# Windowed attention and a gated MLP on one core: the Wo load and the Q reads move to other places in one DMA queue

## The chip, the cores and the metric

The kernel runs on one core of a Trainium2 chip. The metric is the device time of one execution in microseconds (us). A profile is one execution taken by the hardware profiler; its span goes from the first to the last instruction of the program. In what follows PE is the matmul engine and PEld its weight loads, DVE the vector engine, ACT the scalar engine, POOL the GpSimd engine. SP is the engine that only issues DMAs and waits for semaphores: here nearly all DMAs go through its queue, in the order of the program, and while it waits for one of them everything behind it stands.

## What is computed

One block of a transformer on 2048 rows of 640 columns, in bf16: a layernorm, then attention with 32 heads of 20 columns in which each row sees the 256 rows up to and with itself, and beside it a gated MLP of width 1536. Both are added to the input.

```python
def _A_ref(x, wqkv, wo):
    qkv = (x @ wqkv).reshape(B, S, 3, H, Dh).transpose(2, 0, 3, 1, 4)
    q, k, v = qkv[0], qkv[1], qkv[2]
    scores = jnp.einsum("bhqd,bhkd->bhqk", q, k) * (Dh ** -0.5)
    mask = (idx[:, None] - idx[None, :] >= 0) & (idx[:, None] - idx[None, :] < W)
    p = _softmax(jnp.where(mask[None, None], scores, -1e9), axis=-1)
    o = jnp.einsum("bhqk,bhkd->bhqd", p, v)
    return o.transpose(0, 2, 1, 3).reshape(B, S, D) @ wo

def _B_ref(x, w_gate, w_up, w_down):
    h = _sigmoid(einsum("bsd,df->bsf", x, w_gate)) * einsum("bsd,df->bsf", x, w_up)
    return jnp.einsum("bsf,fd->bsd", h, w_down)

xn = _layernorm(x)
return x + _A_ref(xn, wqkv, wo) + _B_ref(xn, w_gate, w_up, w_down)
```

## The kernel before

The rows are cut into four chunks of 512. For each chunk the kernel makes, on PE, the projections to Q and K (`g_qk`, L366: five blocks `m` of 128 columns for Q, then five for K), the projection to V (`g_v`, L385), the gate and up products of the MLP (`g_gu`, L407), and at the end the down product and the output projection with Wo (`g_out`, L463, with `down`, L430, and `add_wo`, L437). The attention runs in steps of scores (`scores`, L480) and exponentials, followed two steps later by the product with V (`pv`, L508). A class `Fill` (L551) holds the other work as generators and deals it out between the score steps, so that PE always has something to do; the list of parts is at L689 to L707. The order of all instructions on each engine is thereby written out by the program itself; `tc.manual_schedule()` (L132) leaves it so, and adds only the semaphore waits.

Q and K come out of PE as 32 heads of 20 rows in a packed layout, and the scores need every head on partitions of its own. So each block goes through memory. `proj_block` (L292) copies a PSUM block to a tile `st` (Q on DVE, L301; K on ACT, L303) and stores it to a scratch tensor in device memory, `sq` or `sk` (L305). `spread` (L307) reads the scratch back into the tiles `qT` and `kT` (L315), two groups of four heads in each DMA of 256 KB. A read must wait until the stores that it reads have landed. A chunk has ten stores, four reads for the first half of the heads and four for the second half.

Wo needs its rows in another order as well: `turn_wo` (L209) writes them to the scratch tensor `wo_i`, and `load_wo` (L215) reads them into the tile `wo`, in four DMAs of 200 KB, one for each quarter of the partitions. The first matmuls that read `wo` are those of L439 in the output part of the first chunk.

The order of DMAs in SP's queue around the change, for the second chunk (c = 1):

- four stores of Q, the four loads of `wo` (L375), the fifth store of Q, two stores of K
- the two reads of `qT` for the first half (L377, yielded behind block m = 1 of K), three stores of K
- the two reads of `kT` for the first half (L393, L394, issued in `g_v`), then two of `qT` and two of `kT` for the second half (L396, L397)
- two loads of input rows (`new_rows`, L449, which the output part of the first chunk starts with)

For the third and fourth chunk it is the same without the loads of `wo`. The first chunk has an order of its own (L379 to L383, L195).

Each DMA that SP issues takes one of eight semaphores in turn, so a DMA also waits for the one issued eight places before it, where that is not known to have landed.

The programs of the engines are themselves in device memory and are brought in by DMA: in the page's list of queues these are the ones of kind "instruction".

Of the kernel before, what the change touches and what calls it, by code (L numbers as in the profile page):

```python
# [15 lines left out]
DC = D // P  # L16
# [77 lines left out]
def kernel(  # L94
# [42 lines left out]
    def load_x(c):  # L137
        t = xp.tile([P, SBC, D], BF16, name="xc")
        xc[c] = t
        nc.sync.dma_start(out=t, in_=xr[:, c * SBC:(c + 1) * SBC, :])  # L140
# [39 lines left out]
    def load_gu(t, w, k, lo=0, hi=FS):  # L180
        nc.sync.dma_start(out=t[k][:, :, lo:hi],
                          in_=w.rearrange("(c p) f -> p c f", p=P)[:, :, k * FS + lo:k * FS + hi])
# [32 lines left out]
    def load_wo():  # L215
        for i in range(HG):
            nc.sync.dma_start(out=wo[32 * i:32 * i + 32, :, :],
                              in_=wo_i[i].rearrange("(m j) n -> j m n", j=32))
# [73 lines left out]
    def proj_block(w, c, m):  # L292

        ps = ps_d.tile([P, CW], FP32, name="pqk", tag="d")
        for d in range(DC):
            wt = wqkv["qk".index(w)][:, d, :].rearrange("p (k m) -> p m k", m=DC)
            nc.tensor.matmul(ps, lhsT=wt[:, m, :], rhs=xnT[c][:, d, :],  # L297
                             start=(d == 0), stop=(d == DC - 1))
        st = stp.tile([P, CW], BF16, name="st")
        if w == "q":  # L300
            nc.vector.tensor_copy(out=st, in_=ps)  # L301
        else:
            nc.scalar.copy(out=st, in_=ps)  # L303
        dst = scratch[w, c % 2].rearrange("(h j) s -> h j s", j=32)
        nc.sync.dma_start(out=dst[:, 4 * m:4 * m + 4, :], in_=st)  # L305

    def spread(w, c, g0, g1):  # L307

        half, first = divmod(g0, GH)
        if first == 0:  # L310
            qk[w, c, half] = (qp if w == "q" else kp).tile([P, GH, CW], BF16, name=w + "T")
        src = scratch[w, c % 2].rearrange("(a b p) s -> b p a s", a=2, p=P)
        for b in range(g0 // 2, g1 // 2):
            o = 2 * b - half * GH
            nc.sync.dma_start(out=qk[w, c, half][:, o:o + 2, :], in_=src[b])  # L315

    def new_v(c, s):
        v = vp.tile([P, 2, VH], BF16, name="v")
        vt[c * SBC + s] = v
        nc.gpsimd.memset(v[:, :, 0:16 * VW].rearrange("p k (h d) -> p k h d", d=VW)[:, :, :, DH:VW], 0.5)  # L320
        nc.gpsimd.memset(v[:, :, 16 * VW:], 0.0)
# [16 lines left out]
    def proj_v(c, s, hf, copy):  # L338
        copy_v(c, s, hf, project_v(c, s, hf), copy)
# [26 lines left out]
    def g_qk(c):  # L366
        for w in "qk":
            for m in range(DC):
                proj_block(w, c, m)
                if c == 0 and w == "q" and m == 1:  # L370
                    load_x(1)
                if c == 0 and w == "q" and m == 3:
                    load_gu(wu, B_w_up, 0, FS // 2)
                if c == 1 and w == "q" and m == 3:
                    load_wo()  # L375
                if c and w == "k" and m == 1:
                    spread("q", c, 0, GH)  # L377
                yield 5 * MM
        if c == 0:  # L379
            spread("q", c, 0, 2)  # L380
            spread("k", c, 0, 2)
            spread("q", c, 2, 4)
            spread("k", c, 2, 4)  # L383

    def g_v(c):  # L385
        for s in range(SBC):
            new_v(c, s)
            for hf in range(2):
                proj_v(c, s, hf, nc.scalar.copy if hf else nc.vector.tensor_copy)
                if hf == 0:  # L390
                    yield 5 * 136
            if s == 0:
                spread("k", c, 0, 2)  # L393
                spread("k", c, 2, GH)  # L394
            if s == 1:
                spread("q", c, GH, NG)  # L396
                spread("k", c, GH, NG)  # L397
            yield 5 * 136


# [271 lines left out]
    for _ in g_qk(0):  # L672
        pass
# [19 lines left out]
    fill.add("wd", later(load_wd), 0)  # L693
    fill.add("pads", later(clear_next), 0)
    fill.add("qk1", g_qk(1), 50 * MM)
    fill.add("v1", mix(g_v(1), g_gu(1, 0, 2), 1, 2), 40 * 136 + 2 * GU)
    fill.add("out0", mix(g_out(0, g_gu(1, 2, 3)), norms2, 1, 1), OUT + GU)
    fill.add("x3", later(load_x, 3), 0)
    fill.add("qk2", g_qk(2), 50 * MM)
    fill.add("v2", mix(g_v(2), g_gu(1, 3, 7), 0, 1), 40 * 136 + 4 * GU)  # L700
    fill.add("gu1b", mix(g_gu(1, 7, 12), norms3, 0, 1, False), 5 * GU)
    fill.add("out1", mix(g_out(1, g_gu(2, 0, 1)), itertools.chain(norms3, g_turns(3)), 1, 2), OUT + GU)
    fill.add("qk3", g_qk(3), 50 * MM)
    fill.add("v3", mix(g_v(3), g_gu(2, 1, 5), 0, 1), 40 * 136 + 4 * GU)
    fill.add("gu2", g_gu(2, 5, 12), 7 * GU)
    fill.add("out2", g_out(2, (), g_gu(3, 0, 1)), OUT + GU)
# [37 lines left out]
    c = NCH - 1  # L744
# [62 lines left out]
```

## Time and profile before

| | us |
|---|---|
| median of three runs | 309.28 |
| lowest and highest of them | 309.27, 309.58 |
| the profiled execution, its own time | 309.91 |
| its span | 308.2 |

| engine | busy, us | share of the span |
|---|---|---|
| PE | 300.0 | 97% |
| ACT | 198.4 | 64% |
| DVE | 170.7 | 55% |
| POOL | 168.7 | 55% |

The granted clock of TensorE is 1.000 over the whole span. The DMA engines move 35.68 MB, 116 GB/s in the mean; by the page's 40 slices they are loaded to 4 to 9 tenths nearly throughout the first 85 us, and after that in bursts, with slices of 0 to 7 tenths. The wait table lists 3.3 us of waits on PE, 2.4 us of them on the warm-up and the transposes at the start (L232, L279). Since PE is busy to 97%, the table of engines says little more; what is of interest is the few places where PE stands, and the time of each DMA in SP's queue, which the timeline gives by its issue.

### The profile page before, as it was taken

To read this page: it belongs to the slowest core of one execution; us is meant where nothing else is said; L and a number is where in the kernel's file an instruction comes from. 1 tells how busy PE (TensorE), PEld (TensorE's weight loads), DVE (VectorE), ACT (ScalarE), POOL (GpSimd) and SP (SyncE) were. 2 spreads that over 40 slices of the span, in tenths; PEclk is the share of its full clock that TensorE was granted. 3 is DMA by queue.
4 is the path that set the end of the run, shared out by engine and by line. 5 is a ranking of instruction groups with operands and counts; after the bars stand their busy time and mean duration, and the time that the engine had idled before them with its cause. 6 is when DMAs were issued, how large, how long until landed. Compare 5 with 4: busy or idle time off the path is not lost.

```text
span 308.2 us, 9938 instructions
## 1 busy us (share of the span) xinstructions
PE 300.0 (97%) x4276; PEld 167.5 (54%) x4311; DVE 170.7 (55%) x339; ACT 198.4 (64%) x197; POOL 168.7 (55%) x308
## 2 busy tenths in 40 slices
PE   6999999999999999999999999999999999999995
PEld 2654444545556655554557664554546664444774
DVE  4733657648698364496947154383734536373423
ACT  5933777698854549888674647878585547678000
POOL 6000687687873937666682728557372837566000
PEclk9999999999999999999999999999999999999999
DMA  7997996984707353730002712650000200000202
GB/s 223 366 307 236 325 174 188 356 231 137 245 3 132 64 178 103 219 100 2 3 3 66 130 57 71 204 184 0 3 2 2 82 31 21 2 2 2 87 21 67
DMA packets 40460, 35.68 MB, mean 116 GB/s; under 512 B 10560, under 2 KB 39872, under 8 KB 40384
## 3 DMA queue, kind: packets, MB, share of 16 engines
q1 hardware_dynamic: 39552, 34.27, 37.8%
q10 hardware_dynamic: 864, 0.77, 0.8%
q8 instruction: 34, 0.56, 0.7%
q14 instruction: 10, 0.08, 0.1%
HBM read 23.63 MB, written 10.26 MB: 110 GB/s over the span
## 4 chain that ended last, share of the span: by engine, by line
PE 96%; DMA 1%; issue 1%; DVE 1%; ACT 0%; SPq 0%
PE y L432 18%; PE pu L418 17%; PE pg L411 17%; PE pqk L297 14%; PE ps L487 9%; PE pv L326 7%; PE y L439 7%; PE acc L520 6%; DMA xc<-in_A_x_dram 1%; PE pt L279 0%; ACT xn L617 0%; DVE xn L272 0%; DVE xn L628 0%; DVE stats L252 0%; SPq L156 0%
## 5 line engine op out<-in xcount | busy, mean ns | idle before, releaser
L504 POOL TENSOR_SCALAR_AFFINE_SELECT pT<-pT 64x512 bf16<-64x512 bf16 (+1 forms) x256 | 157.2, 614 | 109.8 <-ACT pT L493 97.3
L493 ACT ACTIVATE pT<-ps 128x2048 bf16<-128x2048 f32 (+1 forms) x76 | 141.0, 1855 | 59.9 <-PE ps L487 58.1
L422 DVE SCALAR_TENSOR_TENSOR h<-th,pu 128x512 bf16<-128x512 f32 x48 | 32.8, 683 | 52.9 <-PE pu L418 46.3
L418 PE MATMUL pu<-xnT,wu 128*128 128x512 bf16 x228 | 59.0, 380 | 0.7 <-issue 0.2
L411 PE MATMUL pg<-xnT,wg 128*128 128x512 bf16 x226 | 58.5, 380 | 0.9 <-issue 0.3
L432 PE MATMUL y<-wd,h 128*128 128x320 bf16 (+2 forms) x396 | 56.8, 295 | 0.2 <-issue 0.2
L432 PEld LDWEIGHTS <-h 128*128 128x128 bf16 x396 | 36.7, 98 | 16.1 <-issue 2.3
L414 ACT ACTIVATE th<-pg 128x512 f32<-128x512 f32 x48 | 28.6, 595 | 15.5 <-PE pg L411 15.4
L411 PEld LDWEIGHTS <-wg 128*128 128x128 bf16 x240 | 22.3, 98 | 25.8 <-issue 2.0
L418 PEld LDWEIGHTS <-wu 128*128 128x128 bf16 x240 | 22.0, 98 | 25.5 <-issue 2.0
L487 PE MATMUL ps<-qT,kT 20*64 20x320 bf16 (+4 forms) x1440 | 32.1, 260 | 0.0
L532 DVE STREAM_TRANSPOSE t<-acc 128x512 f32<-128x512 f32 x32 | 21.1, 696 | 19.4 <-PE acc L520 19.2
L487 PEld LDWEIGHTS <-kT 20*64 20x64 bf16 x1440 | 15.4, 103 | 24.8 <-issue 21.8
L443 DVE SCALAR_TENSOR_TENSOR rows<-y,rows 128x320 bf16<-128x320 f32 x30 | 14.4, 488 | 25.5 <-PE y L439 25.4
L544 DVE TENSOR_TENSOR on<-t,rec 128x320 bf16<-128x320 f32 (+4 forms) x48 | 27.8, 579 | 1.1
L326 PE MATMUL pv<-wv,xnT 128*128 128x320 bf16 x160 | 25.8, 300 | 0.0
L439 PE MATMUL y<-wo,oc 128*128 128x320 bf16 (+2 forms) x165 | 24.2, 295 | 0.0
L297 PE MATMUL pqk<-xnT,wk 128*128 128x512 bf16 x97 | 23.1, 381 | 0.2
L297 PE MATMUL pqk<-xnT,wq 128*128 128x512 bf16 x94 | 22.8, 381 | 0.4 <-issue 0.2
L335 DVE CAST v<-pv 64x320 bf16<-64x320 f32 x29 | 14.1, 486 | 12.5 <-PE pv L326 12.3
L520 PE MATMUL acc<-pT,v 64*32 64x320 bf16 (+4 forms) x1440 | 19.7, 253 | 0.0
L520 PEld LDWEIGHTS <-v 64*32 64x32 bf16 x1440 | 16.2, 91 | 5.8 <-ACT pT L493 1.7
(50 smaller groups left out, 178.7 us busy)
## 6 DMA issues: line engine op xcount, KB each, us to landing
qT<-sq SPq DMA_DIRECT2D x16, 256.0 KB
kT<-sk SPq DMA_DIRECT2D x16, 256.0 KB
sq<-st SPq DMA_DIRECT2D x20, 128.0 KB
sk<-st SPq DMA_DIRECT2D x20, 128.0 KB
out_dram<-rows SPq DMA_DIRECT2D x15, 160.0 KB
wg<-in_B_w_gate_dram SPq DMA_DIRECT2D x4, 480.0 KB
wu<-in_B_w_up_dram SPq DMA_DIRECT2D x4, 480.0 KB
xc<-in_A_x_dram SPq DMA_DIRECT2D x3, 640.0 KB
```

The lines of the kernel that those rows point to most:

```text
L297: nc.tensor.matmul(ps, lhsT=wt[:, m, :], rhs=xnT[c][:, d, :], start=(d == 0), stop=(d == DC - 1))
L326: nc.tensor.matmul(ps[:, 0:HALF], lhsT=xnT[c][:, d, s * P:(s + 1) * P], rhs=wqkv[2][:, d, hf * HALF:(hf + 1) * HALF], start=(d == 0), stop ...
L411: nc.tensor.matmul(pg, lhsT=part(wg, d, f), rhs=xnT[c][:, d, :], start=(d == 0), stop=(d == DC - 1))
L414: nc.scalar.activation(out=th, in_=pg, func=TANH, scale=0.5)
L418: nc.tensor.matmul(pu, lhsT=part(wu, d, f), rhs=xnT[c][:, d, :], start=(d == 0), stop=(d == DC - 1))
L422: nc.vector.scalar_tensor_tensor(out=h, in0=th, scalar=1.0, in1=pu, op0=ADD, op1=MULT)
L432: nc.tensor.matmul(y[:, 0:cut[1] - cut[0]], lhsT=ht[c, f][:, s * P:(s + 1) * P], rhs=wd[:, f, cut[0]:cut[1]], start=(f == 0), stop=False)
L439: nc.tensor.matmul(y[:, 0:cut[1] - cut[0]], lhsT=oc[c, m][:, s * P:(s + 1) * P], rhs=wo[:, m, cut[0]:cut[1]], start=False, stop=(m == DC - 1))
L487: nc.tensor.matmul(ps[a * U:(a + 1) * U, i, col * U:(col + n) * U], lhsT=qk["k", kc, o // GH][32 * i:32 * i + DH, o % GH + a, kb * U:(kb + ...
L493: nc.scalar.activation(out=pt[:, :, 0:width], in_=ps[:, :, 0:width], func=EXP, scale=SCALE)
L504: nc.gpsimd.affine_select(out=view, in_=view, pattern=[[0, HG], [0, n], [sign, U]], compare_op=GE, fill=0.0, base=base, channel_multiplier ...
L520: nc.tensor.matmul(acc[32 * i:32 * i + 32, q * U:(q + n) * U], lhsT=vt[kb][a * U:(a + 1) * U, u, h * VW:h * VW + 32], rhs=pt[a * U:(a + 1) ...
```

## The change

It moves two things in SP's queue and adds and removes nothing. The loads of `wo` go from behind the fourth Q store of the second chunk to behind all eight reads of its `qT` and `kT`. The reads of the first half of `qT`, in the second, third and fourth chunk, go from behind the second K store to behind the fifth and last.

```diff
@@ g_qk
                 if c == 0 and w == "q" and m == 3:
                     load_gu(wu, B_w_up, 0, FS // 2)
-                if c == 1 and w == "q" and m == 3:
-                    load_wo()
-                if c and w == "k" and m == 1:
+                if c and w == "k" and m == DC - 1:
                     spread("q", c, 0, GH)
                 yield 5 * MM
@@ g_v
             if s == 1:
                 spread("q", c, GH, NG)
                 spread("k", c, GH, NG)
+                if c == 1:
+                    load_wo()
             yield 5 * 136
```

In the built program the order of the instructions on PE, DVE, ACT and POOL is the same as before; SP's order differs as the diff says, and the numbers of the semaphores that are waited for are dealt out anew.

## The prediction

> **What bounds the kernel now.** First the page: the engines, the list of DMA queues (the line kept here is the one that counts later: packets, MB, share) and the chain that ended last.
>
> ```profile
> PE 300.0 (97%) x4276; PEld 167.5 (54%) x4311; DVE 170.7 (55%) x339; ACT 198.4 (64%) x197; POOL 168.7 (55%) x308
> ...
> q8 instruction: 34, 0.56, 0.7%
> ...
> PE 96%; DMA 1%; issue 1%; DVE 1%; ACT 0%; SPq 0%
> ```
>
> PE sets the end. Work that the change takes off a DMA queue is therefore worth only the time for which PE stood still for it. So I next read the waits, for those that a DMA ends behind the start, and then PE's timeline in the second chunk for any break in the row of matmuls.
>
> ```profile
> PEld L487 <- DMA kT<-sk: 0.4, 1, 0.4
> ...
> PE y L432 <- issue: 0.2, 1, 0.2
> ```
>
> ```profile
> 82.43 0.43 PE L487 MATMUL ps<-qT,kT 20*64 20x320 bf16 x24
> 82.79 1.94 PE L432 MATMUL y<-wd,h 128*128 128x320 bf16 x13
> 84.91 1.67 PE L432 MATMUL y<-wd,h 128*128 128x320 bf16 x11 [0.18 <-issue]
> ```
>
> The wait for kT (78.56 us) costs PE nothing: the scores start 0.31 us behind the start of the last gate matmul, as they do at all 18 such places. The kT that they need landed at 78.47, 0.09 us ahead. The other line is a real stop. Matmuls of L432 start every 0.136 us; the 13th starts at 84.43, so the next was due at 84.57 and came at 84.91 (its weight load at 84.90): 0.34 us lost, with no semaphore behind it.
>
> That stop is PE's own program arriving late. Queue q8 brings 34 blocks of 16 KB, for 4276 + 4311 PE instructions: one block per 253 of them, so a block is about 256 instructions, and 34 x 253 is PE's whole program. Asking the DMA view for short windows places each block. Those in stretches with no other traffic (141.35, 148.29, 157.72, 218.93, 223.82 us) start 1.0 to 1.2 us behind the 150th instruction of each 256 (two for each weight load, plus the sequencer's own rows): the sequencer, some 44 instructions ahead of the matmuls, enters one block and orders the next but one. By the same count the block of interest was ordered at 78.04, and started at 82.40, 4.4 us later. The window view shows what lay between (window, length, PE, PEld, DVE, ACT, POOL busy, clock, DMA share, GB/s):
>
> ```profile
> 78.04:82.40 4.36, 4.36 (x114) 2.57 (x112) 1.66 (x3) 4.12 (x7) 3.64 (x10) 1.00 0.94 309
> 82.40:86.01 3.61, 3.43 (x54) 2.27 (x47) 3.42 (x7) 1.88 (x1) 2.96 (x7) 1.00 0.22 74
> ```
>
> The block waited until the reads issued before it had drained, took 1.0 us, and PE went on 2.5 us after its start; the block after it started at 86.01, 1.1 us behind PE's restart. Two others waited in the same way: ordered at 130.1 and started at 133.55, when the traffic had drained; ordered at 199.8 and started at 202.67, when about five of the six reads under way had. So a block stands behind what SP had issued when it was ordered. For each block I took the time at which PE passes its end less (start + 2.45 us): the slack is 0.05 us here, 1.8 for the block of 126.32, 1.3 for that of 202.67, 5.7 for that of 70.61.
>
> By the Trainium skill (DMA: Bandwidth & Descriptors, section Queues, rings and completion order) each DMA engine goes round robin between the queue rows that have work, packet by packet. By that rule a block would not queue behind another row's backlog and the sum below would be nothing; the 4.4 us speak against it here.
>
> **The change, part by part.** SP's queue as it is (start, duration, count):
>
> ```profile
> 62.62 0.52 SPq L305 DMA_DIRECT2D sq<-st  x1
> 63.19 2.15 SPq L217 DMA_DIRECT2D wo<-wo_i  x4
> 65.44 0.52 SPq L305 DMA_DIRECT2D sq<-st  x1
> 66.06 1.24 SPq L305 DMA_DIRECT2D sk<-st  x2
> 70.17 2.06 SPq L315 DMA_DIRECT2D qT<-sq  x2
> 72.33 1.82 SPq L305 DMA_DIRECT2D sk<-st  x3
> 75.74 0.89 SPq L315 DMA_DIRECT2D kT<-sk  x2
> 76.67 0.98 SPq L315 DMA_DIRECT2D qT<-sq  x2
> 77.70 0.98 SPq L315 DMA_DIRECT2D kT<-sk  x2
> 78.72 1.22 SPq L449 DMA_DIRECT2D rows<-in_A_x_dram  x2
> ```
>
> From 66.66 to 70.17 SP stands for the fifth Q store, which landed 4.7 us after its issue behind the wo loads; the last three K stores stand behind that wait.
>
> *Wo away from the Q stores.* The fifth Q tile is copied by 65.16 (DVE, 64.48 + 0.68), so its store moves hardly, by 0.2 us; it lands earlier, for the 0.82 MB of wo no longer lie ahead.
>
> *Q reads behind the K stores.* Nothing waits in front of the K stores now but their copies on ACT, which end in pairs at 67.1 and 69.9 (66.03 + 1.08, 68.74 + 1.12). The last K store goes at 70.0 instead of 73.59. The two qT reads follow at 70.5 to 71.5 inside the 2.15 us that kT waits for that store (73.59 to 75.74 now), so kT goes at 72.15, 3.6 us earlier. PE had not waited for it: gain 0.09 us of margin and no time. If that cover went, with kT later than now, PE would wait for scores one to one; nothing in the new order makes it later.
>
> *Wo behind the reads.* Six reads of 0.47 to 0.50 us bring SP to 75.1, the four wo loads (2.15) to 77.2, the two loads of rows (1.22) to 78.4, each having its semaphore free by then (eight places back are reads that land by 77.3). The first matmul on wo is at 89.48; wo lands by 83 to 84, so this is hidden by 5 us, and the rows are issued 1.5 us earlier than now.
>
> But all of this is now issued by 78.04 to 78.4, ahead of PE's block: 6 x 0.262 + 0.819 + 2 x 0.164 = 2.72 MB, starting 1.3 us behind the issue (as 75.74 to 77.05 now), at 73.45. Before, 1.62 MB had moved from 77.05 to 82.40, 303 GB/s. At that rate the 2.72 MB end at 82.4; at the 259 GB/s of 64.5 to 68.8, when wo moved among stores, at 84.0. I take the middle, 83.2. PE would go on at 83.2 + 2.45 = 85.65 instead of the 84.57 at which it could: 1.1 us of stop for 0.34, **plus 0.75 us**. Bounds: the block behind the reads and wo but not the rows, at 303 GB/s: 81.3, no stop, -0.34 us. All of it, with wo and rows at the 197 GB/s of the 66 to 67 us window: 78.65 + 4.15 + 1.65 = 84.45, PE at 86.9, +2.0 us; +2.25 if SP is a quarter us later.
>
> *Third and fourth chunk.* Only the Q reads move. Third: the last K store goes at 123.3 as now, the qT reads fall into kT's wait (123.9 to 125.5), and kT stays at 125.5; 0.52 MB lie ahead of the block of 126.32 then, at most 0.7 us, of a slack of 1.8. Fourth: K stores no longer stand behind qT (192.84), kT goes about 1.6 us earlier than 197.45; more is issued by 199.8, the block of 202.67 starts at 203.2 (1.90 MB from 197.1 at 311 GB/s), 0.5 us of a slack of 1.3. Both nothing; at 260 GB/s the latter costs 0.4 us, within the range.
>
> PE stays the bound to the end, with all later blocks' slack at 0.66 us or more, so the stop comes through whole. The profiled execution would show a span of 308.2 + 0.75 = 308.95 (its own time, 309.91, is 0.63 above the median). On the median: **309.28 + 0.8 = 310.1 us**.
>
> **The rivals.**
>
> *No change, 309.3 us.* The block is served as early as now: behind the reads and part of wo alone, or in turn with them. For it: a total at the fast rate ends at 82.4, the same as now, and the block of 202.67 started with a read and the rows outstanding. Against: the block of 133.55 waited for nearly all. By the Trainium skill (Runtime: NRT & Kernel Launch, section Instruction fetch mechanics) crossing a 16 KiB block is mostly hidden, with room for 2048 instructions in PE's case; that would make this rival certain. The trace shows a lead of one block only.
>
> *Faster, 308.6 us.* kT's 0.09 us is a tie that runs without a profile may lose: 0.31 us between the lowest and the highest run could be that wait, in all of them in the median's case. Then 0.34 (no stop) + 0.31 = 0.65 us are won. Against: the profiled run lost nothing there, and 309.27 and 309.28 agree.
>
> *The Q reads come too late.* They wait for no more than Q stores that landed 3 us before, and go ahead of kT; PE would have to wait at 78.56 for a qT issued at 70.5. Price if so: each us of lateness past 78.56, thus 311.3 us for a qT that takes 10 us to land. I give it 1 in 50. *That wo is late* at 89.48 needs 5 us more and gets no chance of its own.
>
> **How the numbers follow.** Slower through the program block 0.60 and late reads 0.02; no change 0.28; faster 0.10. 0.2% is 0.62 us, about what a measurement of this kernel can tell from no change; the slower case passes it when the block starts behind 83.05. So faster 0.10, same 0.28, slower 0.62. The forecast's own range is 309.7 to 311.3; with the no-change case and part of the faster one, 308.9 to 311.4.
>
> **What would show it.** Right: kT issued near 72, wo at 75 to 77, the q8 packet of 82.40 moved to 83 or later, and the stop among the L432 matmuls at 84.57 grown to about 1.1 us, with PE unbroken elsewhere. Wrong: the packet at 82.4 or sooner, or a stop that does not follow it; a PE wait at L487 for qT or kT; PE unbroken and the time still longer.

## The result, and the profile after

The changed kernel takes 310.24 us (median of 19 runs, 309.21 to 312.88) against 309.58 for the kernel before (19 runs beside it, 309.07 to 311.38). The ratio is 1.0032, with a 95% interval of 1.0018 to 1.0045: slower by 0.6 to 1.4 us. The span of the profiled execution went from 308.2 to 309.1 us.

The chain of the page after is still PE, and "issue" is still 1% of it:

```profile
PE 302.9 (98%) x4311; PEld 167.7 (54%) x4311; DVE 170.5 (55%) x339; ACT 198.4 (64%) x197; POOL 168.7 (55%) x308
...
PE 96%; DMA 1%; DVE 1%; issue 1%; ACT 0%; SPq 0%
```

PE's busy time is larger (more matmul records are in this trace: all 4311), so shares show nothing here. SP's timeline after (start, duration, count):

```profile
62.18 3.09 SPq L305 DMA_DIRECT2D sq<-st  x2
65.36 4.77 SPq L305 DMA_DIRECT2D sk<-st  x5
70.23 1.69 SPq L315 DMA_DIRECT2D qT<-sq  x2
72.65 0.87 SPq L315 DMA_DIRECT2D kT<-sk  x2
73.57 0.98 SPq L315 DMA_DIRECT2D qT<-sq  x2
74.59 0.98 SPq L315 DMA_DIRECT2D kT<-sk  x2
75.61 1.90 SPq L217 DMA_DIRECT2D wo<-wo_i  x4
77.76 1.09 SPq L449 DMA_DIRECT2D rows<-in_A_x_dram  x2
```

The gap from 66.66 to 70.17 is gone, the K stores run through, kT goes 3.1 us earlier, and from there the reads, wo and the rows follow each other closely up to 78.85. PE's timeline, and the list of what PE waited for behind the start, which now has one line:

```profile
82.34 1.94 PE L432 MATMUL y<-wd,h 128*128 128x320 bf16 x13
85.74 1.67 PE L432 MATMUL y<-wd,h 128*128 128x320 bf16 x11 [1.46 <-issue]
```

```profile
PE y L432 <- issue: 1.5, 1, 1.5
```

It is the same pair of matmuls as before. The 13th starts at 83.98, the 14th was due at 84.11 and came at 85.74: a stop of 1.62 us, where it was 0.34. PE's block of program, by the short windows of the DMA view, started at 82.92 (82.40 before), though PE reached the place of the order 0.4 us sooner, at 77.6. The window from 82.9 to 83.0 (a packet's whole time counts where it starts, so a share can pass 100%):

```profile
q1 hardware_dynamic: 23, 0.02, 105.3%
q8 instruction: 1, 0.02, 83.4%
```

And what went ahead of it, in windows (after the engines: clock, DMA share, GB/s):

```profile
77.00:78.00 1.00, 1.00 (x6) 0.34 (x4) 0.46 (x1) 0.98 (x2) 0.83 (x5) 1.00 1.05 345
78.00:79.00 1.00, 1.00 (x29) 0.69 (x29) 0.00 (x0) 0.96 (x3) 0.94 (x2) 1.00 1.06 351
79.00:80.00 1.00, 1.00 (x9) 0.68 (x7) 0.62 (x2) 1.00 (x2) 0.87 (x3) 1.00 1.14 286
80.00:81.00 1.00, 1.00 (x6) 0.29 (x3) 0.36 (x1) 0.97 (x2) 0.62 (x3) 1.00 1.10 196
...
82.00:83.00 1.00, 1.00 (x37) 0.77 (x30) 0.93 (x2) 0.39 (x1) 0.95 (x2) 1.00 1.20 232
```

The last three columns tell it: the reads move 350 GB/s, and from 79.5 us on, when wo has its turn, the engines are at least as busy (share 1.1 to 1.2) and move 196 to 250.

### The profile page after: what moved, and what is told of

It reads as the page before. It is cut to its first block, busy times and chain, and to the rows that moved or that the text cites. A ratio compares the mean times of both kernels' runs of the same rounds, so it can differ in the third digit from the quotient of the medians.

```text
span 309.1 us, 9980 instructions
## 1 busy us (share of the span) xinstructions
PE 302.9 (98%) x4311; PEld 167.7 (54%) x4311; DVE 170.5 (55%) x339; ACT 198.4 (64%) x197; POOL 168.7 (55%) x308
## 4 chain that ended last, share of the span: by engine, by line
PE 96%; DMA 1%; DVE 1%; issue 1%; ACT 0%; SPq 0%
PE y L432 18%; PE pu L418 17%; PE pg L411 17%; PE pqk L297 15%; PE ps L487 9%; PE pv L326 7%; PE y L439 7%; PE acc L520 6%; DMA xc<-in_A_x_dram 1%; PE pt L279 0%; ACT xn L617 0%; DVE xn L272 0%; DVE xn L628 0%; DVE stats L252 0%; SPq L156 0%
## 5 line engine op out<-in xcount | busy, mean ns | idle before, releaser
L418 PE MATMUL pu<-xnT,wu 128*128 128x512 bf16 x240 | 59.8, 380 | 0.0
L411 PE MATMUL pg<-xnT,wg 128*128 128x512 bf16 x240 | 59.8, 380 | 0.0
L432 PE MATMUL y<-wd,h 128*128 128x320 bf16 (+2 forms) x396 | 56.8, 296 | 1.5 <-issue 1.5
L432 PEld LDWEIGHTS <-h 128*128 128x128 bf16 x396 | 36.6, 98 | 17.4 <-issue 3.6
L411 PEld LDWEIGHTS <-wg 128*128 128x128 bf16 x240 | 22.2, 98 | 25.8 <-issue 2.0
L487 PE MATMUL ps<-qT,kT 20*64 20x320 bf16 (+4 forms) x1440 | 32.1, 260 | 0.0
L487 PEld LDWEIGHTS <-kT 20*64 20x64 bf16 x1440 | 15.4, 103 | 24.8 <-issue 22.2
L439 PE MATMUL y<-wo,oc 128*128 128x320 bf16 (+2 forms) x165 | 24.2, 296 | 0.0
```

Source lines behind the costliest of these rows:

```text
L411: nc.tensor.matmul(pg, lhsT=part(wg, d, f), rhs=xnT[c][:, d, :], start=(d == 0), stop=(d == DC - 1))
L418: nc.tensor.matmul(pu, lhsT=part(wu, d, f), rhs=xnT[c][:, d, :], start=(d == 0), stop=(d == DC - 1))
L432: nc.tensor.matmul(y[:, 0:cut[1] - cut[0]], lhsT=ht[c, f][:, s * P:(s + 1) * P], rhs=wd[:, f, cut[0]:cut[1]], start=(f == 0), stop=False)
L439: nc.tensor.matmul(y[:, 0:cut[1] - cut[0]], lhsT=oc[c, m][:, s * P:(s + 1) * P], rhs=wo[:, m, cut[0]:cut[1]], start=False, stop=(m == DC - 1))
L487: nc.tensor.matmul(ps[a * U:(a + 1) * U, i, col * U:(col + n) * U], lhsT=qk["k", kc, o // GH][32 * i:32 * i + DH, o % GH + a, kb * U:(kb + ...
```

## The experiments

A measure that stays free of the start serves all of them: the time from the first score matmul to the start of the last matmul, from each trace. Beside it stands the stop that the trace shows, less the usual distance of those matmuls.

| run | first score, us | first score to last matmul, us | stop, us, and where |
|---|---|---|---|
| before, first profile | 30.86 | 273.72 | 0.34 at 84.4, L432 |
| before, second | 30.67 | 273.39 | none |
| after, first profile | 30.37 | 275.11 | 1.62 at 84.0, L432 |
| after, second | 30.59 | 274.65 | 1.19 at 84.2, L432 |
| Q reads alone moved | 30.35 | 273.38 | none |
| wo alone moved, first | 32.55 | 273.48 | none |
| wo alone moved, second | 30.35 | 275.73 | 2.28 at 83.9, L432 |
| half of wo, first | 32.22 | 275.25 | 1.86 at 85.8, L432 |
| half of wo, second | 30.35 | 273.69 | 0.26, spread, L432 |
| after, shift 36 | 32.04 | 275.03 | 1.55 at 205.3, L487 |
| after, shift 80 | 30.35 | 274.41 | 1.01 at 202.2, L411 |
| after, shift 128 | 32.10 | 273.38 | none |
| after, shift 128, full warm-up | 30.64 | 273.37 | none |

(With half of wo the line numbers are two higher; L432 stands for the same matmuls.) The stretch is 273.4 us plus the stop in every row, to within 0.1 us. So nothing else between the first score and the last matmul changed by more than that with any of these kernels.

**One part of the change alone.** First the loads of wo without the Q reads:

```diff
-                if c and w == "k" and m == DC - 1:
+                if c and w == "k" and m == 1:
                     spread("q", c, 0, GH)
```

> Only the wo loads move behind the eight reads; the first-half Q reads stay behind the second K store. Theory (PE's program block queues behind all DMAs that SP issued before it was ordered): with wo out of the way of the fifth Q store, kT still goes at about 72.5 us, wo at 75 to 77, so 2.7 MB still lie ahead of the block ordered at 78; it starts at 82.9 as in the changed kernel (82.92), the stop among the L432 matmuls is 1.0 to 1.8 us (1.62 in the changed kernel, 0.34 before), the time 0.5 to 1.2 us above before. Rival (the late Q reads are what costs): the stop stays near 0.34 us and the time within 0.3 us of before.

310.43 us against 309.18, ratio 1.004 (1.0028 to 1.0052). The time came 1.25 us above before, just past the 0.5 to 1.2 us expected, but the profiled execution had none of the stop, so this time can't be put down to it: there the start was 2 us longer. SP also issued wo only from 78.95 on, and by the count PE ordered its block at 79.7, so most of wo came behind the order; the block started at 83.55, and PE needed it at 86.35. The run was repeated for a profile with a usual start.

> The wo loads alone moved, once more, since its first profile fell on an execution whose start was 2 us longer and showed no stop, while its times were 1.2 us above before. Theory: with a usual start (first score at 30.3 to 30.9 us) there is a stop of 0.5 to 1.8 us among the L432 matmuls near 84 us. Rival: no stop, and the time is lost elsewhere in the row of matmuls.

A stop of 2.28 us, more than expected; PE's block started at 83.42.

```profile
82.27 1.94 PE L432 MATMUL y<-wd,h 128*128 128x320 bf16 x13
86.33 1.67 PE L432 MATMUL y<-wd,h 128*128 128x320 bf16 x11 [2.12 <-issue]
```

The ten times spread from 308.88 to 311.47 (ratio 1.0007, 0.9983 to 1.0031, beside runs of before that spread as well), which settles nothing on the time alone. The profile shows that wo alone can bring the stop; with one profile of two it isn't shown how often it does.

Then the Q reads without wo, the kernel before with one line changed:

```diff
-                if c and w == "k" and m == 1:
+                if c and w == "k" and m == DC - 1:
                     spread("q", c, 0, GH)
```

> Only the first-half Q reads move behind the K stores; the wo loads stay among the Q stores. Theory: kT goes at about 72.5 us, the six reads and the two loads of rows (1.9 MB) have drained by about 80, so the block ordered at 78 starts by 80.5 and PE does not stop at all: 0.3 us faster than before (0.0 to 0.6). Rival (the late Q reads are what costs): a stop of over 1 us, at L487 or at L432, and the time 0.6 us above before.

309.23 us against 309.18, ratio 1.0006 (0.9995 to 1.0016); PE's block started at 80.42 and PE did not stop. The late Q reads cost nothing. The gain of 0.3 us did not come; a likely reason showed later: the second profile of the kernel before has no stop to win back.

**Once more the two kernels**, for a second profile of each.

> The changed kernel once more, for its profile: theory, the stop among the L432 matmuls of the second chunk again at 1.0 to 2.0 us (1.62 in the first profile) and the block before it started at 82.5 to 83.5 us; if the stop is a chance of the one profile, it is 0.4 us or less here.

> The kernel before once more, for its profile: the first one showed a stop of 0.34 us at 84.57 and a time 0.63 us above the median. If that stop is usual it is 0.2 to 0.5 us here; if most executions have none, PE's row of L432 matmuls is unbroken and the span about 307.5 us.

After: the stop again, 1.19 us, with the block started at 82.49. PE's timeline of this run:

```profile
82.94 1.52 PE L432 MATMUL y<-wd,h 128*128 128x320 bf16 x10
85.48 1.67 PE L432 MATMUL y<-wd,h 128*128 128x320 bf16 x11 [1.02 <-issue]
```

Before: no stop, the block started at 81.69, and the row of L432 is in one piece:

```profile
82.64 3.43 PE L432 MATMUL y<-wd,h 128*128 128x320 bf16 x24
```

**PE's program moved against the work, DMAs untouched.** These runs make the case for the program block. Some wide warm-up matmuls at the start are replaced by more, narrow ones, so that the ends of the blocks fall on other work; every DMA is issued in the order of the changed kernel.

```diff
-    for n in (6, 4):
+    for n, wide in ((6, CW), (44, U)):
         ps = ps_d.tile([P, CW], FP32, name="pwarm", tag="d")
         for k in range(n):
-            nc.tensor.matmul(ps, lhsT=ones[:, 0:P], rhs=ones, ...)
+            nc.tensor.matmul(ps[:, 0:wide], lhsT=ones[:, 0:P], rhs=ones[:, 0:wide], ...)
```

The pairs are ((6, CW), (44, U)) for a shift of 80 instructions, ((6, CW), (22, U)) for 36, ((2, CW), (72, 32)) and ((5, CW), (69, 32)) for 128.

> The changed kernel, with its DMA order untouched; the last four warm-up matmuls on PE are replaced by 44 narrow ones, so that every later PE instruction stands 80 places further on in PE's program and the ends of its blocks fall 80 instructions earlier in the work. Theory: the block that was ordered at 77.6 us is ordered at about 75 and passed before it is needed; by the count from the changed kernel's trace the least slack of any block is 1.3 to 1.5 us, so there is no stop among the L432 matmuls at 84 or elsewhere: 1.6 us faster than the changed kernel, 0.2 to 0.6 us faster than before. Rival (wo or the Q reads delay PE through data or bandwidth, not through its program): the stop of 1.6 us stays at the same matmuls.

310.65 us, ratio to before 1.0038 (1.0026 to 1.005). The stop at 84 us went, and the forecast was still wrong: another came at 202 us, in the fourth chunk, where a block started at 200.97 behind that chunk's reads.

```profile
202.15 0.38 PE L411 MATMUL pg<-xnT,wg 128*128 128x512 bf16 x1
203.38 0.82 PE L411 MATMUL pg<-xnT,wg 128*128 128x512 bf16 x3 [0.85 <-issue]
```

> As the run before, with 22 narrow matmuls, a shift of 36 places. Theory: the stop at 84 us goes (slack 1.2 us there), and another appears in the fourth chunk, near 205 us, where a block is then ordered just as the reads of that chunk and the rows have been issued: 0.6 to 1.6 us there. The time comes out 0.2 us below to 0.8 us above before. Rival: the stop stays at 84 us, and nothing appears near 205.

The stop went from L432 to the scores near 205 us, as foretold, and took 1.55 us:

```profile
205.08 0.41 PE L487 MATMUL ps<-qT,kT 20*64 20x320 bf16 x18
206.86 0.23 PE L487 MATMUL ps<-qT,kT 20*64 20x64 bf16 x6 [1.37 <-issue]
```

The time, 311.59 us (ratio 1.0061, 1.0042 to 1.008), is 1.6 us above what was expected: the first score, at 32.04 us, is 1.7 us later in the profile than the usual 30.35. The warm-up is a little shorter here (its last matmul starts at 4.49 us instead of 4.63), but the second profile with wo alone had a usual start with 4.44, so why the start is longer is not shown.

> The changed kernel with a shift of 128 places: eight of the ten warm-up matmuls are replaced by 72 narrow ones (32 columns). The two shifts before moved the stop from 84 us to 202 and 205 us; by the count from their traces a shift of 128 has no block whose end is reached less than 1.0 us after it is there. Theory: no stop anywhere, and the time within 0.4 us of before, 0.6 to 1.2 us faster than the changed kernel, with the DMA order of the change untouched. Rival (the new DMA order costs through something besides PE's program): the time stays 0.6 us or more above before though PE's program is never late.

No stop anywhere, and 273.38 us from the first score to the last matmul, as without the change. But the time was 310.5 us (ratio 1.0028, 1.0007 to 1.0048); in the profile the start was 1.5 us longer. The windows of the start, 8 to 10 us, of this run and of the next, count 11 and 18 matmuls:

```profile
8.00:10.00 2.00, 2.00 (x11) 1.26 (x10) 0.75 (x2) 1.89 (x7) 0.00 (x0) 1.00 1.06 382
```

```profile
8.00:10.00 2.00, 1.86 (x18) 1.30 (x16) 1.49 (x5) 1.89 (x7) 0.00 (x0) 1.00 1.06 378
```

> The changed kernel with a shift of 128 places again, now with five wide and 69 narrow warm-up matmuls, so that the warm-up ends near 4.7 us as in the unshifted kernels. In the shift of 128 before, PE was never late for its program and the stretch from the first score matmul to the last matmul was that of the kernel before (273.39 us each), but the start took 1.5 us longer because the warm-up ended at 3.6 us. Theory: with the start restored the whole gain shows in the time: within 0.3 us of before, 0.6 to 1.2 us faster than the changed kernel; first score at 30.3 to 30.8 us, no stop. Rival (the new DMA order costs elsewhere): 0.6 us or more above before with no stop in the profile.

309.27 us against 309.63, ratio 0.9993 (0.9976 to 1.001): with all DMAs of the change in their new places, and only PE's instructions counted off differently, the loss is gone. PE's timeline shows the 24 matmuls of L432 in one piece, and PE waits for nothing behind the start:

```profile
82.57 3.43 PE L432 MATMUL y<-wd,h 128*128 128x320 bf16 x24
```

It isn't shown to beat the kernel before; there is nothing left for PE to win at these places.

The traces also give the place of every stop in PE's program, counting two for each weight load with its matmul and one for each other row of PE. Before the first instruction behind the stop stand 1985 others in both profiles of the changed kernel, in the first of the kernel before, in the second with wo alone and in the first with half of wo; with the shifts of 36 and 80 it is 5825. Both are 193 more than a multiple of 256, and 5825 lies 15 blocks of 256 behind 1985. So PE stops at the same place of a block each time, whether L432, L487 or L411 stands there.

**Half of the load.** Two of the four wo loads back among the Q stores (`load_wo` now takes the first and last of the loads to make):

```diff
+                if c == 1 and w == "q" and m == 3:
+                    load_wo(0, 2)
...
                 if c == 1:
-                    load_wo()
+                    load_wo(2, HG)
```

> The changed kernel with two of the four wo loads (0.41 of 0.82 MB) put back among the Q stores. Theory: the block ordered at 77.6 us starts 1.3 to 1.6 us sooner than in the changed kernel (82.92), at 81.3 to 81.6, and the stop of 1.62 us shrinks to 0.0 to 0.5 us; the time is 0.0 to 0.5 us above before. Rival (where wo stands does not matter, the Q reads do): stop and time as in the changed kernel.

> Half of wo moved, once more, since its first profile fell on an execution with a start 1.6 us longer and showed a stop of 1.86 us where 0.0 to 0.5 was expected. Theory: with a usual start the stop is 0.0 to 0.8 us; if it is again over 1.2 us, half of wo is enough to hold the block and the amount moved does not set the stop.

The first profile missed: a stop of 1.86 us, in an execution whose start was 1.6 us longer. The second met it: the block started at 81.72, and 24 matmuls of L432 took 3.69 us, where 3.43 is usual. The median of 12 runs is 310.05 us (ratio 1.0017, 0.999 to 1.0044), which is not clear of either kernel. That the amount of wo ahead of the block counts is thus plausible, but these two profiles don't show it.

## Why the prediction was right, step by step

**The step that bears it**, PE's block behind what SP has issued, held: the stop grew at the place named, wo alone can bring it, the Q reads alone don't, and a shift of PE's program moves it or takes it away with the DMAs untouched. The packet moved later, to 82.92 and 82.49, though not to the "83 or later" of the forecast. By the places of the stops, a block that PE orders is the next one behind the block it enters; the prediction's words, "the next but one", are wrong, but its times were read from the trace and don't hang on them.

**Its size** was about right, with errors that met in the middle. Foretold was a stop of 83.2 + 2.45 - 84.57 = 1.1 us; measured were 82.92 + 2.82 - 84.11 = 1.62 and 82.49 + 2.99 - 84.29 = 1.19. The drain was foretold at one rate, the middle between 303 and 259 GB/s, to the end of the rows. The mean from 73.45 to 82.92 was 277 GB/s, close to that, but as a mixture of reads at 350 and wo at about 200, and the block did not wait for the rows: in the first profile 0.3 MB, about their size, moved after it had started, in the second more. That 83.2 was nearly hit is thus partly luck. From the start of the block to PE's restart it took 2.8 and 3.0 us, not 2.45, and PE was due earlier than in the profile that the forecast started from.

**The credit of 0.34 us** was doubtful. The first profile's stop was subtracted as if every execution had it; the second has none. The span grew by 0.9 us from first to first profile and by 1.0 from second to second; 0.75 had been foretold. On the medians it is 0.66 us, by the ratio 0.6 to 1.4.

**SP's new order** was right to half a microsecond: kT 72.15 foretold, 72.65 measured; wo 75.1 to 77.2, and 75.6 to 77.5; rows issued to 78.4, and 78.85. Wo behind the reads was hidden for its reader: the waits listed for L439 are the same as before (0.8 us in 4 of its weight loads, none of them for a DMA).

**Third and fourth chunk**, put at nothing, cost nothing. PE itself ran 0.9 us later there than in the first profile of before. Less that, the block of 126.32, now at 128.54, moved by 1.3 us (at most 0.7 foretold), with 0.45 us of slack left; that of 202.67, now at 204.10, moved by 0.5 us, as foretold, with 0.8 us left.

**The rivals.** *No change* fell by the interval. *Faster*, on kT's 0.09 us, fell with the Q reads alone, where kT goes at 73.29 (75.74 before) and the time is the same. *The Q reads too late* fell with the same run. By the Trainium skill (DMA: Bandwidth & Descriptors, section Queues, rings and completion order) a row of its own would be served in turn with the others; the block after the change started 5.3 us behind its order, with traffic on the other row all the while, so the trace again speaks against it. By the Trainium skill (Runtime: NRT & Kernel Launch, section Instruction fetch mechanics) PE holds 2048 instructions; PE came to a stand each time at the end of the block ahead of the late one, thus with a lead of one block of 256, and this speaks against 2048.

## What to carry to other kernels

A load that is hidden for its reader can still cost time: an engine's own program is brought in by DMA too, and in the changed kernel a block of it started 5.3 us after its order when data was issued ahead of it, against 1.0 to 1.2 us where no other traffic ran. Where an engine runs hundreds of short instructions in a few microseconds, its next block can be due in the middle of a burst. When the busiest engine stops for "issue" with no semaphore behind it, look at which transfers were issued before the last block of its program, and either move bulk out of that burst or move the block's end (here a shift of 128 instructions did it). Since any added instruction moves all later ends, such a stop may come or go with edits that have nothing to do with it (36 and 80 instructions more moved it from 84 to 205 and 202 us).

## What had not been expected

- The four wo loads, which write 32 partitions each, move about 200 GB/s with all DMA engines busy (196 at a share of 1.10); the reads of `qT` and `kT`, on 128 partitions, move 350. Whether the partitions are the reason was not tried.
- In some executions the start is 1.5 to 2.2 us longer, also with kernels whose start is the same: with wo alone moved, the first score came at 32.55 us in one profile and at 30.35 in the other. In the first, the granted clock was 0.50 from 8 to 10 us. In three others with a long start (half of wo, and the shifts of 36 and 128) the granted clock is 1.00 and PE still made 10 to 12 matmuls in those 2 us instead of 18 or 19. With a warm-up whose last matmul starts at 3.6 us instead of 4.6 all twelve runs took 309.94 us or more. What starts it in the unchanged start stays open.
- The stop varies between executions of one kernel: 0 and 2.28 us in the two profiles with wo alone, 1.62 and 1.19 with the changed kernel. This may be why the changed kernel's 19 runs spread over 3.7 us and those of before over 2.3.
